# A fused retention and SwiGLU kernel: the last three down-projections by seven products in place of eight

## The chip, the cores and the metric

The kernel runs on one core of one Trainium2 chip. The metric is the device time of one execution in microseconds (us). Before the change it is 229.09 us, the median of three runs (229.01 to 229.27). The profile is one execution of the same program, with a span of 227.3 us from its first to its last instruction.

The engines are named as the profile names them: PE is TensorE (PEld its weight loads), DVE is VectorE, ACT is ScalarE, POOL is GpSimd, SP is SyncE, which here only issues DMAs (SPq).

## What is computed

A retention layer (a decayed running state per head) whose output goes through an RMS norm and a gated feed-forward layer. Sizes: 4 sequences, 8 heads, 768 positions, head size 64; then 3072 tokens of 512 features, with 1536 hidden features.

```python
for t in range(S):
    state = gamma * state + einsum('bhd,bhe->bhde', k[:, :, t], v[:, :, t])
    y[:, :, t] = scale * einsum('bhd,bhde->bhe', q[:, :, t], state)
x = y.transpose(0, 2, 1, 3).reshape(3072, 512)
xn = x / sqrt(mean(x * x, -1) + 1e-6) * rms_g
g, val = xn @ w_gate, xn @ w_val            # 512 -> 1536
out = (g * sigmoid(g) * val) @ w_out        # 1536 -> 512
```

## The kernel before

The sequence of 768 positions is cut into 6 groups of 128 positions; a group holds all 4 sequences, so 512 tokens. For each group the kernel makes the retention output, the norm, and the feed-forward layer, and work of neighbouring groups is interleaved.

The order of all of it is written out in one string, ORDER. Each word is one small operation: its name, its group, its sequence or pair of sequences and its parts; after "/" the PSUM banks (0 to 7) that it writes, after "@" the engine. The words are issued in that order, each engine works through its own in order, and a layer below puts in semaphores where one operation needs another's data or its buffer. The words that matter here:

- Retention of groups 2 to 5, by pairs of sequences: k multiplies keys and values into kv_ps (L485), u0 and u1 add it to the state (VectorE, L490 and L494), b0 and b1 cast the state. z starts y_ps with the state (L506), a makes the scores a_ps (L462), m0 and m1 mask them into am (VectorE, L471), and w adds scores times values to y_ps (L522, L506).
- Norm: S squares and sums y_ps on ScalarE (L567), R makes rstd on GpSimd (L581, L583), N makes xn on VectorE (L595), and XE transposes it by a DMA from SP's queue into xnT (L614). y_ps keeps its bank until N has read it.
- Feed-forward: g and v are products of 4 matmuls of 512 columns for one slice of 128 hidden features (L665), s the silu on ScalarE (L676), h the product of both on VectorE into hT (L686 for groups 2 to 5). hT holds the 1536 hidden features as 12 slices of 128 by 512 tokens.
- Down-projection: d multiplies 128 tokens of hT with w_out, 12 matmuls of 512 columns into one bank (L695), so 48 matmuls a group; e does the last 128 tokens of group 5 in three pieces of 192, 192 and 128 columns (L721). o copies the bank to o_sb on ScalarE or VectorE (L142), and st stores it from SP's queue (L710, L712).
- V, Cq: scaled copies of the values and queries as they arrive (L383, L364), on VectorE or GpSimd.

In the order of before, the down-projections of groups 2 and 3 stand between group 4's w and its first g, where the norm and the transposes of group 4 run on the other engines.

Of the kernel before, what the change touches and what calls it, by code (L numbers as in the profile page):

```python
# [54 lines left out]
v.2.6.7.0.4/4 g.2.7.8.0.4/5 g.2.5.6.0.4/3 g.2.4.5.0.4/6 v.2.1.2.0.4/0 R.3.0 R.3.1 h.2.6.7.0.4 N.3.1 Cq.3.2@P
h.2.1.2.0.4 N.3.0 V.3.2@P s.2.8.9.0.4 s.2.7.8.0.4 s.2.5.6.0.4 g.2.0.1.0.4/5 v.2.7.8.0.4/1 v.2.8.9.0.4/2 v.2.5.6.0.4/3
g.2.2.3.0.4/0 k.3.1/47 tq.3.3 tk.3.3 tk.3.2 Lv.4.2@S tq.3.2 Lv.5.2@S Lq.5.3@S XE.3.1@S Lq.4.0@S Cq.5.3@P V.4.2@D
h.2.5.6.0.4 h.2.7.8.0.4 u0.3.1 h.2.8.9.0.4 s.2.4.5.0.4 s.2.2.3.0.4 b0.3.1@A s.2.0.1.0.4 v.2.0.1.0.4/3 v.2.4.5.0.4/1
v.2.2.3.0.4/2 z.3.1/50 a.3.1/46 u1.3.1 h.2.4.5.0.4 m0.3.1 m1.3.1 h.2.0.1.0.4 Cq.5.2@D h.2.2.3.0.4 g.2.10.11.0.4/1
v.2.9.10.0.4/4 w.3.1 g.2.9.10.0.4/3 v.2.11.12.0.4/6 v.2.10.11.0.4/2 g.2.11.12.0.4/7 S.3.2 s.2.9.10.0.4 S.3.3  # L60
s.2.10.11.0.4 s.2.11.12.0.4 Lk.4.3@P R.3.2 R.3.3 N.3.2 h.2.9.10.0.4 N.3.3 h.2.10.11.0.4 h.2.11.12.0.4 Lv.5.3@S
XE.3.0@S tq.4.1 Lv.4.0@S st.0.0@S XE.3.2@S Lv.4.1@S XE.3.3@S st.0.1@S Lv.4.3@S Lq.4.2@S d.2.1.0.10/4 d.2.1.10.12
d.2.2.0.12/6 d.2.3.0.12/2 g.3.11.12.0.4/7 v.3.0.1.0.4/0 g.3.0.1.0.4/1 g.3.6.7.0.4/5 g.3.10.11.0.4/3 st.0.3@S Lq.4.3@S
tk.4.0 st.1.0@S o.2.3@A s.3.6.7.0.4 o.2.2@A s.3.0.1.0.4 V.5.3@D o.2.1@A V.4.3@D h.3.0.1.0.4 V.4.1@P s.3.11.12.0.4
s.3.10.11.0.4 g.3.3.4.0.4/5 g.3.2.3.0.4/6 v.3.11.12.0.4/4 v.3.10.11.0.4/3 v.3.6.7.0.4/7 g.3.4.5.0.4/0 v.3.3.4.0.4/1
g.3.1.2.0.4/2 Cq.4.3@D h.3.10.11.0.4 h.3.11.12.0.4 V.4.0@D h.3.6.7.0.4 s.3.3.4.0.4 s.3.4.5.0.4 s.3.1.2.0.4 Cq.4.2@P
# [30 lines left out]
def kernel(  # L97
# [11 lines left out]
    nc = tc.nc  # L109
# [88 lines left out]
    def ring(shape, dtype, name, bufs):  # L198
        return sb.tile(shape, dtype, name=name, bufs=bufs)
# [506 lines left out]
    def st(e, bk, c, b, i=None):  # L706
# [4 lines left out]
        else:  # L711
            e.dma_start(out=out_h[c, b // 2, b % 2][:, :, m], in_=x)  # L712


    CUT = (0, 192, 384, 512)

    @op
    def e(e, bk, c, b, i):
# [42 lines left out]
```

## Time and profile before

| what | us |
|---|---|
| median of three runs | 229.09 |
| span of the profiled execution | 227.3 |
| PE busy | 221.2 |
| DVE busy | 121.5 |
| ACT busy | 88.0 |
| POOL busy | 88.2 |

A row of the chain is: start, length, engine, tile and line, with the count of merged instructions. A row of the timeline is: start, length, engine, line, operation and its tiles. A row of a group ends with its busy time, the mean length of one instruction in ns, and the idle time in front of it with what ended that. How busy PE and DVE were in 40 equal slices of the span, in tenths:

```profile
PE   7899999999999999999999999999999999999994
DVE  6495459946388685247751377850564543052211
```

### The profile page before, as it was taken

Reading aid. Unit: us, or ns where it says so; the run is one execution under the profiler, and the core shown is the slowest. Engines: PE = TensorE matmul, PEld = TensorE weight load, DVE = VectorE, ACT = ScalarE, POOL = GpSimd, SP = SyncE. Lnnn points to the kernel's source line nnn. Section 1 sums busy time; section 2 is a strip of 40 time slices with the busy share of each in tenths; the row PEclk is TensorE's granted clock in tenths of the full one; section 3 lists DMA queues with packets and bytes.
Section 4 is the critical chain, followed back from the end, with each engine's and each line's share of the span. In section 5 each row is a group of like instructions: output and inputs, shape, how many; then the busy total and the mean of one; then the engine's idle time right before and its main releaser. Section 6 shows DMA issues by size and latency. Waiting matters only on the chain.

```text
span 227.3 us, 5786 instructions
## 1 busy us (share of the span) xinstructions
PE 221.2 (97%) x2410; PEld 115.0 (51%) x2410; DVE 121.5 (53%) x224; ACT 88.0 (39%) x192; POOL 88.2 (39%) x137
## 2 busy tenths in 40 slices
PE   7899999999999999999999999999999999999994
PEld 2577854565455644444444445544554444444453
DVE  6495459946388685247751377850564543052211
ACT  7798323341525540724411545251452232152011
POOL 8899897746632640743225803170031000000000
PEclk9999999999999999999999999999999999999999
DMA  6999999999999986999969999556003400220116
GB/s 130 174 164 180 197 172 193 177 187 200 186 145 159 182 119 146 248 143 219 154 163 257 163 159 218 130 102 136 2 6 87 144 0 4 91 92 0 46 52 227
DMA packets 105355, 31.57 MB, mean 139 GB/s; under 512 B 94449, under 2 KB 102385, under 8 KB 105330
## 3 DMA queue, kind: packets, MB, share of 16 engines
q0 software_dynamic: 40112, 9.70, 46.4%
q1 hardware_dynamic: 65218, 21.51, 44.1%
q8 instruction: 19, 0.31, 0.6%
q14 instruction: 6, 0.05, 0.1%
HBM read 28.31 MB, written 6.29 MB: 152 GB/s over the span
## 4 chain that ended last, share of the span: by engine, by line
PE 87%; DMA 4%; DVE 2%; issue 2%; POOL 2%; SPq 0%; ACT 0%; POOLq 0%
PE g_ps L665 26%; PE v_ps L665 26%; PE o_ps L695 25%; DMA qb<-in_q_dram 2%; DMA qf<-in_q_dram 2%; PE o_ps L721 1%; DVE am L535 1%; PE kv_ps L485 1%; PE a_ps L428 1%; PE y_ps L522 1%; PE y_ps L506 1%; PE y_ps L550 1%; PE t_ps L396 1%; PE t_ps L391 1%; PE xt_ps L608 1%
## 5 line engine op out<-in xcount | busy, mean ns | idle before, releaser
L665 PE MATMUL v_ps<-xnT,wv_b 128*128 128x512 bf16 (+2 forms) x344 | 70.0, 345 | 0.0
L665 PE MATMUL g_ps<-xnT,wg_b 128*128 128x512 bf16 (+2 forms) x344 | 69.7, 345 | 0.0
L676 ACT ACTIVATE sg<-g_ps 128x512 bf16<-128x512 f32 (+2 forms) x76 | 41.9, 577 | 67.0 <-PE g_ps L665 54.4
L695 PE MATMUL o_ps<-wo_b,hT 128*128 128x512 bf16 x276 | 62.6, 380 | 0.0
L686 DVE TENSOR_TENSOR hT<-sg,v_ps 128x512 bf16<-128x512 bf16 x48 | 32.8, 723 | 38.7 <-ACT sg L676 19.4
L665 PEld LDWEIGHTS <-wv_b 128*128 128x128 bf16 x344 | 30.8, 98 | 30.2 <-DVE hT L686 0.4
L665 PEld LDWEIGHTS <-wg_b 128*128 128x128 bf16 x344 | 30.3, 98 | 29.3 <-DVE st_f L494 0.2
L695 PEld LDWEIGHTS <-hT 128*128 128x128 bf16 x276 | 26.2, 98 | 29.8
L595 DVE SCALAR_TENSOR_TENSOR xn<-y_ps,rstd,g_bc 128x512 bf16<-128x512 f32 x24 | 17.6, 746 | 12.7 <-POOL rstd L583 12.1
L688 DVE TENSOR_TENSOR hT<-sg,v_ps 128x512 bf16<-128x512 bf16 (+2 forms) x28 | 16.6, 606 | 14.6 <-PE v_ps L665 7.5
L364 POOL TENSOR_TENSOR qb<-qf,ydec 128x512 bf16<-128x512 f32 x13 | 13.7, 1065 | 26.9 <-DMA qf<-in_q_dram 26.9
L142 ACT COPY o_sb<-o_ps 128x512 f32<-128x512 f32 (+2 forms) x17 | 9.2, 553 | 36.6 <-PE o_ps L695 32.3
L567 ACT ACTIVATE xsq<-y_ps 128x512 f32<-128x512 f32 x24 | 14.2, 596 | 21.6 <-PE y_ps L506 16.2
L336 POOL DMA_DIRECT2D kb<-in_k_dram x20 | 18.2, 911 | 2.6 <-DMA wo_b<-in_moe_w_out_dram 1.4
L581 POOL TENSOR_SCALAR ms<-ssq 128x1 f32<-128x1 f32 x21 | 4.4, 212 | 35.1 <-ACT xsq L567 30.0
L471 DVE TENSOR_TENSOR am<-a_ps,causal_h 128x512 bf16<-128x512 f32 x16 | 10.6, 684 | 8.9 <-PE a_ps L462 8.9
L142 DVE COPY o_sb<-o_ps 128x512 f32<-128x512 f32 (+1 forms) x9 | 5.7, 647 | 13.8 <-PE v_ps L665 4.8
L583 POOL TENSOR_TENSOR rstd<-ms,mhalf 128x1 f32<-128x1 f32 x21 | 11.6, 551 | 1.7
L535 DVE TENSOR_TENSOR am<-a_ps,mask 128x512 bf16<-128x512 f32 x16 | 10.2, 681 | 2.4 <-PE a_ps L428 2.3
L383 POOL TENSOR_TENSOR vp<-vf,vdec 128x512 bf16<-128x512 f32 x7 | 7.3, 1050 | 7.9 <-DMA vf<-in_v_dram 7.9
L383 DVE TENSOR_TENSOR vp<-vf,vdec 128x512 bf16<-128x512 f32 x9 | 6.2, 692 | 4.5 <-DMA vf<-in_v_dram 4.5
L229 PE MATMUL hot_ps<-one 128*128 128x512 bf16 x16 | 6.2, 523 | 1.0 <-DVE one L149 1.0
(99 smaller groups left out, 166.4 us busy)
## 6 DMA issues: line engine op xcount, KB each, us to landing
out_dram<-o_sb SPq DMA_DIRECT2D x23, 256.0 KB, 2.4
vf<-in_v_dram SPq DMA_DIRECT2D x17, 256.0 KB, 3.6
qf<-in_q_dram SPq DMA_DIRECT2D x16, 256.0 KB, 4.1
kb<-in_k_dram POOLq DMA_DIRECT2D x23, 128.0 KB, 6.1
wo_b<-in_moe_w_out_dram POOLq DMA_DIRECT2D x3, 512.0 KB, 10.7
qb<-in_q_dram POOLq DMA_DIRECT2D x8, 128.0 KB, 7.4
vp<-in_v_dram POOLq DMA_DIRECT2D x7, 128.0 KB, 10.1
wv_b<-in_moe_w_val_dram POOLq DMA_DIRECT2D x3, 256.0 KB, 6.2
```

Source lines behind the costliest of these rows:

```text
L142: return (e.copy if e is ACT else e.tensor_copy)(out, in_)
L336: i = done[n, c, b] = e.dma_start(out=x, in_=rows[n][b, c])
L364: e.tensor_tensor(out=u["qb"], in0=u["qf"], in1=ydec[:, c, :, None].to_broadcast([128, H, D]), op=ALU.mult)
L383: e.tensor_tensor(out=u["vp"], in0=u["vf"], in1=vdec[:, c, :, None].to_broadcast([128, H, D]), op=ALU.mult)
L535: return DVE.tensor_tensor(out=u["am"][:, i], in0=u["a"][i], in1=m, op=ALU.mult)
L567: return ACT.activation(xsq, flat(u["y"]), AF.Square, accum_out=u["ssq"])
L595: return DVE.scalar_tensor_tensor(out=u["xn"], in0=flat(u["y"]), scalar=u["rstd"], in1=g_bc, op0=ALU.mult, op1=ALU.mult)
L665: r = nc.tensor.matmul(p[:, (n - n0) * m:(n - n0 + 1) * m], W[w][0][:, s, n * 128:(n + 1) * 128], xnT[c][:, s, b0 * C:b1 * C], start=s == ...
L676: return ACT.activation(sg[:, :cols], done["wg", c, n0, b0][:, :cols], AF.Silu)
L686: return DVE.tensor_tensor(out=out, in0=sg, in1=p, op=ALU.mult)
L688: return DVE.tensor_tensor(out=hT[c][:, n0:n1, b0 * C:b1 * C], in0=sg, in1=p, op=ALU.mult)
L695: nc.tensor.matmul(o_ps[c, b], hT[c][:, n, b * C:(b + 1) * C], wo_b[:, n, :], start=n == 0, stop=n == NFF - 1)
```

## The change

For groups 3, 4 and 5 the down-projection C = A B (A: 512 tokens by 1536, B: w_out, 1536 by 512) is cut into two by two blocks: A into halves of 256 tokens and of 768 features, B into halves of 768 features and of 256 columns. Strassen's scheme, in Winograd's form, makes the four blocks of C from seven block products in place of eight:

- Sums of B (word tw, once): T1 = B12 - B11, T2 = B22 - T1, T3 = B22 - B12, T4 = B21 - T2. Each is 1536 elements a partition.
- Sums of A (word ss, for each group, in parts by slices): S1 = A21 + A22, S2 = S1 - A11, S3 = A11 - A21, S4 = A12 - S2. S3 and S4 are written over A21 and A12 in hT, S1 and S2 into a buffer, ssum. In groups 3 and 4 a part is 3 slices by 256 tokens (768 elements), in group 5 2 slices (512).
- Products (word p): P1 = A11 B11, P2 = A12 B21, P3 = S4 B22, P4 = A22 T4, P5 = S1 T1, P6 = S2 T2, P7 = S3 T3. Each is 12 matmuls of 256 columns (6 slices by two blocks of 128 tokens); in group 5 each is issued in two halves of 6, by token block.
- Three banks hold the results (word r). P1 is copied out by ScalarE (part), then P2 is added in its bank, which gives C11, copied to o_sb by ScalarE. P6's bank is read with P1 added (part), then takes P7, is read with P1 added (part), then takes P4, and gives C21. P5's bank gives C22, then takes P3 and gives C12. So P2 waits for the copy of P1, P7 and P4 for the two reads of P6's bank, P3 for the reading of C22. These reads are additions on VectorE.

All sums of A and B are bf16 in and out, on VectorE. The sums of B lie where the masks of groups 0 and 1 lay, ssum where their states lay, the parts in other buffers used early. The list ORDER is word for word the same up to group 2's down pieces, but with bank numbers exchanged (1 with 7, 2 with 6, 3 with 5); after that it is written anew. Four of the last eight stores, of 256 columns each, are issued by ScalarE.

```diff
+    def tw(e, bk, i):
+        b11, b12, b21, b22 = (wo_b[:, f, m] for f in (F0, F1) for m in (M0, M1))
+        out, x, y = ((t1, b12, b11), (t2, b22, t1), (t3, b22, b12), (t4, b21, t2))[i - 1]
+        return e.tensor_tensor(out=out, in0=x, in1=y, op=ALU.subtract)
...
+    def ss(e, bk, i, c, n0, n1):
+        (a11, a21), (a12, a22) = ([hT[c][:, f, m] for m in (slice(0, GT // 2), slice(GT // 2, GT))] for f in (slice(n0, n1), f1))
+        out, x, y, f = ((s1, a21, a22, ALU.add), (s2, s1, a11, ALU.subtract), (a21, a11, a21, ALU.subtract),
+                        (a12, a12, s2, ALU.subtract))[i - 1]
+        return e.tensor_tensor(out=out, in0=x, in1=y, op=f)
...
+    def p(e, bk, i, c, j0=0, j1=2, n0=0, n1=NFF // 2):
+        for n in range(n0, n1):
+            l, off, r = {1: (h0, 0, w0[:, :, M0]), 2: (h1, 0, w1[:, :, M0]), 3: (h1, 0, w1[:, :, M1]), 4: (h1, k, t[:, 3]),
+                         5: (None, 1, t[:, 0]), 6: (None, 2, t[:, 1]), 7: (h0, k, t[:, 2])}[i]
+            for j in range(j0, j1):
+                nc.tensor.matmul(x[:, j - j0], z[:, j * C:(j + 1) * C], r[:, n],
+                                 start=i in (1, 5, 6) and n == 0 and j == j0, stop=n == NF2 - 1, skip_group_check=True)
...
+    def r(e, bk, i, c, j0=0, j1=2, j=None):
+        z = {6: 1, 67: 1, 21: 1, 22: 67, 12: 6}.get(i)
+        if i in (1, 6, 67):
+            return copy(e, y, x) if i == 1 else DVE.tensor_tensor(out=y, in0=x, in1=z, op=ALU.add)
+        for n in range(j0, j1):
+            if i == 11:
+                copy(e, y, x[:, n - j0])
+            else:
+                DVE.tensor_tensor(out=y, in0=x[:, n - j0], in1=z[:, n - j0], op=ALU.add)
```

VectorE between the last hT of group 3 and the first hT of group 4, before (am is m0 and m1, xn the norm, both of groups 4 and 5):

```order
L686 TENSOR_TENSOR hT<-sg,v_ps 128x4x2x64 x3
L471 TENSOR_TENSOR am<-a_ps,causal_h 128x512 x2
L595 SCALAR_TENSOR_TENSOR xn<-y_ps,rstd,g_bc 128x512 x4
L364 TENSOR_TENSOR qb<-qf,ydec 128x512
L471 TENSOR_TENSOR am<-a_ps,causal_h 128x512
L490 TENSOR_TENSOR st_m_109<-st_f_107,kv_ps 128x512
L471 TENSOR_TENSOR am<-a_ps,causal_h 128x512
L142 COPY o_sb<-o_ps 128x512
```

And now, up to the last xn of group 4 and the addition behind it:

```order
L692 TENSOR_TENSOR hT<-sg,v_ps 128x4x2x64 x3
L759 TENSOR_TENSOR ssum<-hT 128x768 x2
L759 TENSOR_TENSOR hT<-hT 128x3x256
L477 TENSOR_TENSOR am<-a_ps,causal_h 128x512 x2
L759 TENSOR_TENSOR ssum<-ssum,hT 128x768 x2
L759 TENSOR_TENSOR hT<-hT,ssum 128x3x256
L601 SCALAR_TENSOR_TENSOR xn<-y_ps,rstd,g_bc 128x512
L759 TENSOR_TENSOR hT<-hT,ssum 128x3x256
L788 TENSOR_TENSOR part_3039<-p_ps,part_2936 128x512
L759 TENSOR_TENSOR hT<-hT 128x3x256
L601 SCALAR_TENSOR_TENSOR xn<-y_ps,rstd,g_bc 128x512 x3
L788 TENSOR_TENSOR part_3101<-p_ps,part_2936 128x512
```

All eight sums of group 3 and its first two additions now stand ahead of or between the masks and norms of group 4. On TensorE the same place holds, in this order: P1, z and a of group 4's second pair, P2, w of both pairs, P6, ten matmuls of group 2's d, P7, P5, P4, z and a of group 5, P3, the last two matmuls of that d, w of group 5, then the first g of group 4.

VectorE at the end of the program, before (the last hT of group 5, then copies of the down-projection):

```order
L686 TENSOR_TENSOR hT<-sg,v_ps 128x4x2x64 x11
L142 COPY o_sb<-o_ps 128x512
L686 TENSOR_TENSOR hT<-sg,v_ps 128x4x2x64 x9
L142 COPY o_sb<-o_ps 128x192
L142 COPY o_sb<-o_ps 128x512 x2
```

And now, from the third sum behind the last hT:

```order
L759 TENSOR_TENSOR ssum<-ssum,hT 128x512
L759 TENSOR_TENSOR hT<-hT,ssum 128x2x256 x2
L788 TENSOR_TENSOR part_3039<-p_ps,part_2936 128x256
L759 TENSOR_TENSOR hT<-hT,ssum 128x2x256
L759 TENSOR_TENSOR hT<-hT 128x2x256
L788 TENSOR_TENSOR part_3039<-p_ps,part_2936 128x256
L788 TENSOR_TENSOR part_3101<-p_ps,part_2936 128x256
L797 TENSOR_TENSOR o_sb<-p_ps,part_3101 128x256
L788 TENSOR_TENSOR part_3101<-p_ps,part_2936 128x256
L797 TENSOR_TENSOR o_sb<-p_ps,part_3101 128x256
L797 TENSOR_TENSOR o_sb<-p_ps,part_2936 128x256 x2
L797 TENSOR_TENSOR o_sb<-p_ps,part_3039 128x256 x2
```

Where three copies ended the program, seven sums (two stand ahead of the first row here) and ten additions follow the last hT. On TensorE, 14 half products follow the last v: P1, P1, P2, P2, P6, P6, P5, P7, P7, P5, P4, P4, P3, P3. The down-projection of group 4, which stood there before, is done earlier.

More of the change, by code (lines that the diff above doesn't have):

```diff
@@ new lines @@
+XE.0.0@A g.0.0.2.0.1/2 X.0.1/5 v.0.0.2.0.1/4 Y.0.3/7 tab s.0.0.2.2.3 S.0.3 U.0.0.2@A U.0.2.2@A s.0.0.2.0.1 XE.0.1@D
+Lq.1.1@P R.0.3 h.0.0.2.2.3 h.0.0.2.0.1 N.0.3 mc.0@P g.0.4.5.0.3/5 g.0.5.6.0.3/0 g.0.0.2.1.2/1 v.0.5.6.0.3/6
+v.0.4.5.0.3/2 v.0.0.2.1.2/4 g.0.2.3.0.3/3 X.0.3/7 Lq.1.0@P Lq.1.2@P Lk.1.1@P B.0.1 wg.6.9 Lk.1.3@P s.0.4.5.0.3
+s.0.5.6.0.3 h.0.4.5.0.3 h.0.5.6.0.3 zst.0@P s.0.2.3.0.3 XE.0.3@D s.0.0.2.1.2 v.0.2.3.0.3/2 g.0.3.4.0.3/3 v.0.0.4.3.4/1
+g.0.4.6.3.4/7 g.0.0.4.3.4/6 h.0.0.2.1.2 D.1.0@D h.0.2.3.0.3 s.0.0.4.3.4 s.0.3.4.0.3 s.0.4.6.3.4 v.0.4.6.3.4/2
@@ L93 @@
+ss.3.5.4.6@D r.6.5.1.2 st.5.1.0@S p.5.5.0.1/7 p.7.5.0.1 r.67.5.0.1 p.7.5.1.2 r.22.5.0.1 p.5.5.1.2/3 st.5.0.0@A
+st.5.2.1@A r.67.5.1.2 p.4.5.0.1 r.22.5.1.2 st.5.3.1@A r.21.5.0.1 p.4.5.1.2 p.3.5.1.2 st.5.2.0@S p.3.5.0.1 r.21.5.1.2
+st.5.3.0@S r.12.5.1.2 st.5.1.1@A r.12.5.0.1 st.5.0.1@S
 """
@@ L167 @@
     darg = const.tile([128, NCH, H], F32, name="darg")
-    below = const.tile([128, C], F32, name="below")
     eps = const.tile([128, 1], F32, name="eps")
@@ L172 @@
     ydec = const.tile([128, NCH, H], F32, name="ydec")
-    mask0 = const.tile([128, 2, NHP, C], F32, name="mask0")
-    mask1 = const.tile([128, 2, NHP, C], F32, name="mask1")
-    qdec = const.tile([128, NHP, C], F32, name="qdec")
-    row_m = const.tile([128, C], F32, name="row_m")
+    shared = NFF // 2 * DM
+    early = const.tile([128, shared], F32, name="early", tag="shared")
+    mask0, mask1 = (early[:, i * H * C:(i + 1) * H * C].rearrange("p (i hp c) -> p i hp c", i=2, hp=NHP) for i in range(2))
+    qdec = early[:, 2 * H * C:2 * H * C + NHP * C].rearrange("p (hp c) -> p hp c", hp=NHP)
+    row_m, below = (early[:, 2 * H * C + (NHP + i) * C:2 * H * C + (NHP + i + 1) * C] for i in range(2))
     lngp = const.tile([128, NHP], F32, name="lngp")
@@ L187 @@
     causal_h = const.tile([128, HC], BF16, name="causal_h")
-    st_b = [const.tile([128, NHP, 2 * D], BF16, name=f"st_b{b}") for b in range(B)]
+    st_all = const.tile([128, 6, NHP, 2 * D], BF16, name="st_b", tag="shared_st")
+    st_b = [st_all[:, b] for b in range(B)]
     t = {(c, b): {} for c in range(NCH) for b in range(B)}
@@ L196, in bank, with ring @@
         return psum.tile(shape, dtype, name=name, tag=f"bank{i}")
-    def ring(shape, dtype, name, bufs):
-        return sb.tile(shape, dtype, name=name, bufs=bufs)
+    def ring(shape, dtype, name, bufs, tag=None):
+        return sb.tile(shape, dtype, name=name, bufs=bufs, tag=tag or name)
     def after(i, *what):
@@ L712, in st @@
             e.dma_start(out=out_h[c, b // 2, b % 2][:, :, m], in_=x)
-    CUT = (0, 192, 384, 512)
-    @op
-    def e(e, bk, c, b, i):
-        p = o_ps[c, b, i] = bank(bk[0], [128, CUT[i + 1] - CUT[i]], F32, "o_ps")
-        for n in range(NFF):
-            nc.tensor.matmul(p, hT[c][:, n, b * C:(b + 1) * C], wo_b[:, n, CUT[i]:CUT[i + 1]],
-                             start=n == 0, stop=n == NFF - 1)
+    NF2 = NFF // 2
+    F0, F1 = slice(0, NF2), slice(NF2, NFF)
+    M0, M1 = slice(0, DM // 2), slice(DM // 2, DM)
@@ new lines @@
+    CUT = (0, DM // 2, DM)
+    sums, prod = {}, {}
+    @op
+    def tw(e, bk, i):
+        if "T" not in sums:
+            sums["T"] = const.tile([128, 4, NF2, DM // 2], BF16, name="wsum", tag="shared")
+        b11, b12, b21, b22 = (wo_b[:, f, m] for f in (F0, F1) for m in (M0, M1))
+        t1, t2, t3, t4 = (sums["T"][:, j] for j in range(4))
+        out, x, y = ((t1, b12, b11), (t2, b22, t1), (t3, b22, b12), (t4, b21, t2))[i - 1]
+        return e.tensor_tensor(out=out, in0=x, in1=y, op=ALU.subtract)
@@ new lines, in row_sum, with part @@
+    def row_sum(i, c, n0, n1):
+        if "S" not in sums:
+            sums["S"] = const.tile([128, 2, NF2, GT // 2], BF16, name="ssum", tag="shared_st")
+        return sums["S"][:, i - 1, n0:n1]
+    def part(i):
+        if ("s", i) not in prod:
+            pool, tag = {1: (sb, "kf"), 6: (const, "shared_g"), 67: (const, "part")}[i]
+            prod["s", i] = pool.tile([128, 2, DM // 2], F32, name=f"part{i}", bufs=1, tag=tag)
+        return prod["s", i]
+    @op
+    def ss(e, bk, i, c, n0, n1):
+        f1 = slice(NF2 + n0, NF2 + n1)
+        (a11, a21), (a12, a22) = ([hT[c][:, f, m] for m in (slice(0, GT // 2), slice(GT // 2, GT))] for f in (slice(n0, n1), f1))
+        s1, s2 = row_sum(1, c, n0, n1) if i < 3 else None, row_sum(2, c, n0, n1) if i != 3 and i > 1 else None
+        out, x, y, f = ((s1, a21, a22, ALU.add), (s2, s1, a11, ALU.subtract), (a21, a11, a21, ALU.subtract),
+                        (a12, a12, s2, ALU.subtract))[i - 1]
+        return e.tensor_tensor(out=out, in0=x, in1=y, op=f)
@@ new lines @@
+    INTO = {1: 1, 2: 1, 11: 1, 6: 2, 7: 2, 4: 2, 67: 2, 21: 2, 5: 3, 3: 3, 22: 3, 12: 3}
+    @op
+    def p(e, bk, i, c, j0=0, j1=2, n0=0, n1=NFF // 2):
+        if bk:
+            prod[INTO[i], c, j0] = bank(bk[0], [128, j1 - j0, DM // 2], F32, "p_ps")
+        x, t = prod[INTO[i], c, j0], sums["T"]
+        h0, h1 = hT[c][:, :NF2], hT[c][:, NF2:]
+        w0, w1 = wo_b[:, :NF2], wo_b[:, NF2:]
+        k = GT // 2
+        for n in range(n0, n1):
+            l, off, r = {1: (h0, 0, w0[:, :, M0]), 2: (h1, 0, w1[:, :, M0]), 3: (h1, 0, w1[:, :, M1]), 4: (h1, k, t[:, 3]),
+                         5: (None, 1, t[:, 0]), 6: (None, 2, t[:, 1]), 7: (h0, k, t[:, 2])}[i]
+            z = row_sum(off, c, n, n + 1)[:, 0] if l is None else l[:, n, off:off + k]
+            for j in range(j0, j1):
+                nc.tensor.matmul(x[:, j - j0], z[:, j * C:(j + 1) * C], r[:, n],
+                                 start=i in (1, 5, 6) and n == 0 and j == j0, stop=n == NF2 - 1, skip_group_check=True)
@@ new lines, in r @@
+    @op
+    def r(e, bk, i, c, j0=0, j1=2, j=None):
+        x = prod[INTO[i], c, j0]
+        if j is not None:
+            x, j0, j1 = x[:, j - j0:j - j0 + 1], j, j + 1
+        z = {6: 1, 67: 1, 21: 1, 22: 67, 12: 6}.get(i)
+        z = z and part(z)[:, j0:j1]
+        if i in (1, 6, 67):
+            y = part(i)[:, j0:j1]
+            return copy(e, y, x) if i == 1 else DVE.tensor_tensor(out=y, in0=x, in1=z, op=ALU.add)
+        for n in range(j0, j1):
+            b = 2 * (i // 10 - 1) + n
+            if ("o", c, b) not in done:
+                done["o", c, b] = ring([128, DM], F32, "o_sb", 6)
+            y = done["o", c, b][:, (M0, M1)[i % 10 - 1]]
+            if i == 11:
+                copy(e, y, x[:, n - j0])
+            else:
+                DVE.tensor_tensor(out=y, in0=x[:, n - j0], in1=z[:, n - j0], op=ALU.add)
```

145 lines of the change are left out of this document (71 added, 74 removed).

## The prediction

> **What bounds the kernel now.** I read the page first (engine shares, slices), then TensorE's waits, then the chain that ended last in order of time, then instruction groups by shape and the timeline.
>
> ```profile
> PE 221.2 (97%) x2410; PEld 115.0 (51%) x2410; DVE 121.5 (53%) x224; ACT 88.0 (39%) x192; POOL 88.2 (39%) x137
> PEclk9999999999999999999999999999999999999999
> ```
>
> TensorE (PE) is busy 97% of the span at full granted clock; VectorE (DVE) is half idle. Are the gaps in TensorE real waits? Its waits, whole list:
>
> ```profile
> PE t_ps L391 <- DMA qb<-in_q_dram: 1.1, 1, 1.1
> PE hot_ps L229 <- DVE one L149: 1.0, 1, 1.0
> PE kv_ps L485 <- DVE vp L383: 0.4, 1, 0.4
> ```
>
> 2.5 us in three waits; the last, for vp, lies at 82 us (first row below), ahead of the stretch that changes. So from group 2 on the time is the length of TensorE's stream, and any microsecond taken out of it shows, as long as no new wait comes in. The chain (start, length) gives its prices:
>
> ```profile
> 81.64 0.66 DVE vp L383
> ...
> 144.52 0.38 PE y_ps L522 x32
> 144.90 0.27 PE y_ps L506 x32
> 145.16 0.32 PE a_ps L462 x32
> ...
> 148.68 10.47 PE o_ps L695 x48
> ...
> 184.16 1.73 PE v_ps L665 x8
> ...
> 215.68 0.99 PE o_ps L721 x12
> 216.66 5.61 PE o_ps L695 x26
> 222.28 1.67 PE o_ps L721 x24
> 223.97 0.27 ACT o_sb L142
> ```
>
> A group's down-projection is 48 matmuls 512 wide: 10.47 us, 218 ns each. One v or g product (4 matmuls) is 0.86 us. Twelve matmuls 192 wide take 0.99 us, 82.5 ns each; the last row is twelve of 192 and twelve of 128, so 128 wide is (1.67 - 0.99)/12 = 57 ns.
>
> **TensorE's part.** Three groups go from 48 matmuls of 512 columns to 7 products of 12 matmuls of 256. No row is 256 wide. Between the 192 and 512 rows the slope is (218 - 82.5)/320 = 0.42 ns a column, which puts 256 at 109.6 ns; half of a 512 is 109. So 84 x 109.6 = 9.21 us, a saving of 1.26 us a group, **3.8 us** for three (3.6 to 3.9). Group 5's narrow pieces (0.99 + 1.67 = 2.66 against 12 x 0.218 = 2.62) return 0.04 more. A product is 1.32 us; in group 5, cut in halves, 0.66.
>
> ```profile
> L695 PEld LDWEIGHTS <-hT 128*128 128x128 bf16 x276 | 26.2, 98 | 29.8
> ```
>
> The loading of weights could spoil this, since there are now 84 loads in place of 48. A load's record is 98 ns long beside a 512, but the 192-wide row already issues one each 82.5 ns, so loads hide at 109. The Trainium skill (TensorE: Matmul & The Clock Gate, section Back-to-back issue gap) speaks against the change: it gives a sustained stream 81 ns at 128 wide and 131 at 512, hence about 98 at 256 as an estimate, by which 84 x 98 = 8.2 us would replace 48 x 131 = 6.3. The trace disagrees at both ends, 57 and 218 ns, and the rows decide.
>
> **VectorE's part.** Added are 4 sums of weights (1536 elements a partition), 16 sums of activations of 768 and 12 of 512, all two-byte in SBUF; then 22 additions of 256 and 4 of 512 that read PSUM. Four copies go.
>
> ```profile
> L142 DVE COPY o_sb<-o_ps 128x512 f32<-128x512 f32 x8 | 5.5, 683 | 9.5 <-PE v_ps L665 4.8 <-PE o_ps L695 4.7
> L142 DVE COPY kT<-t_ps 128x512 bf16<-128x512 bf16 x2 | 0.8, 420 | 0.5 <-PE t_ps L396 0.5
> L650 DVE TENSOR_TENSOR st_f<-st_f,kv_ps 128x256 f32<-128x256 f32 x2 | 0.8, 416 | 0.0
> L650 DVE TENSOR_TENSOR st_f<-st_f,kv_ps 128x512 f32<-128x512 f32 x1 | 0.7, 679 | 0.0
> ```
>
> The additions that read PSUM have their rows: 416 and 679 ns, so 22 x 0.416 + 4 x 0.68 = 11.9 us. Those two rows give 1.03 ns an element and 153 ns fixed. No row has a two-input sum with all operands two-byte, so two ends. Upper: the same rate, 0.94 us for 768, 0.68 for 512, 1.73 for 1536, 30 us in all. Lower: the same copy takes 683 ns in four-byte and 420 in two-byte; (420 - 153)/512 = 0.52 ns an element, so 0.55, 0.42 and 0.95 us, 17.7 us in all. Every row at the high rate has a four-byte operand, and the new sums have none, so I take the **lower end** and keep the other as a rival. The Trainium skill (VectorE: DVE Perf Modes, section The perf-mode tier table) has bf16 tensor_tensor in SBUF at twice the fp32 rate, 1224 against 2293 ns for 2048 elements, which as an estimate is 0.56 us for 768 and leads to the same sum; no run here shows it yet.
>
> ```profile
> 120.00:227.00 107.00, 103.94 (x959) 49.95 (x956) 44.19 (x67) 34.55 (x71) 18.59 (x30) 1.00 0.52 100
> ```
>
> Net of the copies (2.4 us) that is 27 us more. From 120 us on VectorE was busy 44 of 107 us (third figure of the row); 71 fits, but it works in order, so place decides.
>
> ```profile
> 115.87 0.67 DVE L383 TENSOR_TENSOR vp<-vf,vdec 128x512 bf16<-128x512 f32 x1
> 120.66 0.69 DVE L383 TENSOR_TENSOR vp<-vf,vdec 128x512 bf16<-128x512 f32 x1 [4.12 <-DMA vf<-in_v_dram]
> 127.28 0.73 DVE L686 TENSOR_TENSOR hT<-sg,v_ps 128x512 bf16<-128x512 bf16 x1 [5.93 <-ACT sg L676]
> ...
> 131.29 0.67 DVE L383 TENSOR_TENSOR vp<-vf,vdec 128x512 bf16<-128x512 f32 x1
> ...
> 138.51 1.95 DVE L686 TENSOR_TENSOR hT<-sg,v_ps 128x512 bf16<-128x512 bf16 x3 [0.31 <-PE v_ps L665]
> ```
>
> The first three rows show where VectorE idled, the last that the gaps between two starts are shorter than the records: three hT products in 1.95 us, about 0.61 a start. I count 0.48 us a start for a 768-sum, 0.34 for a 512-sum, and the full length where a result is waited for.
>
> - *Sums of weights.* They come where VectorE idled 4.1 + 5.9 us; 3.8 (upper end 6.9) fits. Cost nothing.
> - *Group 3's products*, counted from the end of its last v product (zero). TensorE: P1 to 1.32, z and a of group 4 (16 matmuls of L506 and 32 of L462, some 0.5 by the first rows) to 1.8. P2 adds into P1's bank and must wait for ScalarE's copy (0.59 us by the row below, 1.37 to 1.96): 0.15 lost. P2 ends at 3.3, w.4.0 (32 of L522, 16 of L506, 0.5) at 3.8, then w.4.1 needs the second mask product. VectorE: last hT from 0.1, three sums from 0.9, mask products from 2.35 to 3.65. Just in time. The norm then goes w, ScalarE square, GpSimd rstd, VectorE xn:
>
> ```profile
> L142 ACT COPY o_sb<-o_ps 128x512 f32<-128x512 f32 x15 | 8.6, 588 | 33.3 <-PE o_ps L695 32.3 <-DMA out_dram<-o_sb 0.9
> ```
>
> ```profile
> 146.24 0.20 ACT L567 ACTIVATION_READ_ACCUMULATOR xsq<-y_ps 128x1 f32 x1
> 147.40 0.75 DVE L595 SCALAR_TENSOR_TENSOR xn<-y_ps,rstd,g_bc 128x512 bf16<-128x512 f32 x1 [0.49 <-POOL rstd L583]
> 152.36 1.06 POOL L364 TENSOR_TENSOR qb<-qf,ydec 128x512 bf16<-128x512 f32 x1
> 152.77 1.19 DVE L364 TENSOR_TENSOR qb<-qf,ydec 128x512 bf16<-128x512 f32 x1
> ```
>
> ```profile
> L614 SPq DMA_TRANSPOSE xnT<-xn x8: 1189/1215/1711, 149.1 to 176.0; - x8
> DMA to landing us min/median/max: 2.3/2.4/3.6
> ```
>
>   From the end of the accumulator's read to xn is 0.96 us, and the four xn now stand between sums: I get starts at 5.5, 7.7, 8.4 and 9.0. P5's bank holds the third one's y_ps, free at 9.15, wanted at 9.1. After the last xn (9.8) two transposes of about 1.2 us in SP's queue and their landing (2.3 to 3.6, the last row) end at 13.3 to 14.6; TensorE asks for xnT at 14.8. All in all **0.5 us** of stalls (0.2 to 1.5).
> - *Group 4's products* have v and g products of group 5 between them: P2 comes 1.7 us after P1, P7 2.6 us after P6. No stall.
> - *Group 5's products* stand alone at the end, 14 halves of 0.66, 9.2 us. After the last hT (0.1 to 0.8) VectorE has seven sums and one addition ahead of the first P7, which is the eighth half, at 4.6; its last S3 ends at 4.5. P4, at 6.6, wants an addition done at 5.8; the last P3 one done at 7.1, and starts at 7.9. No stall.
> - *The end.* An addition of 256 (0.42) takes the place of a copy of 128 (0.27), and the last store is 128 KB in place of 64; stores of 64, 96 and 256 KB landed 1.9, 2.0 and 2.4 us after issue, so 0.2 more. Together +0.35.
>
> ```profile
> out_dram<-o_sb SPq DMA_DIRECT2D x8, 256.0 KB, 2.4
> out_dram<-o_sb SPq DMA_DIRECT2D x2, 96.0 KB, 2.0
> out_dram<-o_sb SPq DMA_DIRECT2D x1, 64.0 KB, 1.9
> ```
>
> ScalarE loses 8 copies of 512 and two small ones and gets 2 of 512 and 8 of 256, about 1 us less; the four stores it issues stand behind all its other work, so nobody waits for them. The shared buffers reuse space that groups 0 and 1 left long before.
>
> **Sum:** -3.8 - 0.04 + 0.5 + 0.35 = -3.0 us. The profiled span was 227.3 us, so 224.3; the median of 229.09 lies 1.8 us around it, which I leave as it is: **226.1 us**.
>
> **Rivals.**
> 1. *Sums at the four-byte rate (slower).* The sums start 0.4 us later each. In group 3 the second mask product ends at 4.8 in place of 3.65, w.4.1 waits 1 us, and the xn, P7 and P5 behind it come later by turns: some 3 us in all. In group 4, P6's second half and P7 wait for S2 and S3, near 1.5. In group 5, P7 waits 0.6. That is 5 us: **231**. It turns into a loss once a 768-sum takes more than about 0.78 us, where 60% of that is lost. For it: every two-input row here runs at that rate. Against: they all have a four-byte operand.
> 2. *The rate holds but VectorE is late anyway.* Just-in-time places in group 3 slip: an operation with two SBUF inputs took 1.19 us on VectorE while GpSimd ran its own (rows of 152 us), against 0.67 without at 131 us, and GpSimd still has two such loads there. One to two sums so delayed and xnT later by as much: +1 to +2.5, **227.8**.
> 3. *A fixed cost a matmul* that the narrow rows, only 12 or 24 long, hide: TensorE gains nothing. 35 ns a matmul more would take the 1.26 us of a group (36 matmuls more); with the stalls and the end **229.9**. For it stand 84 weight loads; against it 57 and 82.5 ns, whose slope (0.40) leaves 6 ns at zero width. The page on TensorE cited above would have it so.
>
> **How the numbers follow.** Forecast 0.62 (225.0 to 226.9), rival 2 0.18 (227 to 228.6), waits that eat all of the gain 0.06 (within 0.2% of before, about what a measurement can tell from no change), rival 1 0.11, rival 3 0.03. Faster 0.80, same 0.06, slower 0.14. The range takes in the forecast and rival 2: 225.0 to 228.6.
>
> **What would show it.** Right: 252 matmuls of 256 columns, near 109 ns apart; sums of 768 near 0.55 us; TensorE's waits still a few, with ScalarE's copy of P1 among them, together under 1 us more; the chain's end an addition and a store. Wrong: sums near 0.9 us with long waits for ssum and am in group 3 and at the end (rival 1); waits of g_ps for xnT or of P5 for xn at the start of group 4 (rival 2); 84 matmuls taking over 10 us without waits (rival 3).

## The result and the profile after

The changed kernel took **226.32 us**, the median of four runs, beside 229.05 for four runs of the kernel before on the same chip. The ratio is 0.9869 with a 95% interval of 0.9838 to 0.9901, so 3.0 us less (2.3 to 3.7); the medians differ by 2.7. The forecast was 226.1 (225.0 to 228.6). One of the four runs took 230.26: late runs turn up with either list (two of six when the changed kernel ran again, two of eleven of the kernel before beside it), and the ratios leave them out while the medians do not.

The first lines of the page of after, busy time, share and count of each engine, then the granted clock:

```profile
PE 215.6 (96%) x2466; PEld 123.7 (55%) x2494; DVE 148.1 (66%) x278; ACT 87.1 (39%) x192; POOL 88.6 (40%) x137
...
PEclk9999999999999999999999999999999999999998
```

TensorE still fills the span (223.9 us now, 227.3 before), but with 5.6 us less work by the records (28 matmuls of after have none, as the counts of PE and PEld show, so this is somewhat too much). VectorE has 26.6 us more of it; the prediction counted 27. All of TensorE's waits, in us, times, longest:

```profile
PE hot_ps L235 <- DVE one L154: 1.0, 1, 1.0
PE t_ps L397 <- DMA qb<-in_q_dram: 1.0, 1, 1.0
PE o_ps L701 <- issue: 0.6, 4, 0.2
PE v_ps L671 <- issue: 0.3, 2, 0.2
PE kv_ps L491 <- DVE vp L389: 0.3, 1, 0.3
```

The three old waits are there. No wait for a sum, an addition, a mask, a norm or a transpose has come in. New are six short "issue" gaps, together 0.9 us. They are no idle time: in front of each stands a matmul without a record. At 158.1 us, for instance, two weight loads of a d run on PEld, and only one matmul of it is on record (start, length):

```profile
158.07 0.11 PEld L701 LDWEIGHTS <-hT 128*128 128x128 bf16 x2
```

```profile
158.30 0.38 PE L701 MATMUL o_ps<-wo_b,hT 128*128 128x512 bf16 x1 [0.16 <-issue]
```

The chain in order of time (start, length) shows where TensorE's stream changed: group 3's products, group 4's, and the end.

```profile
113.72 5.18 PE o_ps L701 x24
...
144.03 1.31 PE p_ps L776 x12
145.85 0.41 PE y_ps L528 x32
146.42 1.42 PE p_ps L776 x12
147.84 0.37 PE y_ps L528 x32
148.34 1.42 PE p_ps L776 x12
149.81 2.11 PE o_ps L701 x9
151.92 3.93 PE p_ps L776 x36
156.09 0.26 PE a_ps L468 x32
156.35 1.42 PE p_ps L776 x12
...
183.86 1.34 PE p_ps L776 x12
...
186.93 2.62 PE p_ps L776 x24
...
192.14 5.24 PE p_ps L776 x48
...
211.19 9.19 PE p_ps L776 x84
220.40 0.42 DVE o_sb L797
```

Three readings. First, group 5's 84 matmuls of 256 columns took 9.19 us without a break, 109.4 ns each; the forecast had 109.6. Second, in group 3 three of the products took 1.42 us in place of 1.31, and each of those stands right behind small matmuls (y_ps or a_ps, 64 by 64). Third, the first y_ps L528 stands *before* the second p_ps: w of group 4's first pair runs ahead of P2. The sentence ahead of the prediction, that P2 precedes w of both pairs, is wrong, and so is the place of P2 in the prediction's walk through group 3.

The kernel's front part does not change, yet its length differs from profile to profile (113.7 us in after and 114.4 in before, but 118.5 in slow_sums and 116.7 in keys_early, whose profiled executions took 237.72 and 228.64 us). So the profiles are compared by a **stretch**: from the first matmul of group 2's first d to the end of the last matmul. Its start in the chain of before (its last row, 222.28 with 1.67, stands in the prediction):

```profile
114.41 7.77 PE o_ps L695 x36
```

Before: 222.28 + 1.67 - 114.41 = 109.54 us, and 3.35 from there to the end of the span. After: 211.19 + 9.19 - 113.72 = 106.66, and 3.52. So the stretch gained 2.88 and the end lost 0.17, together 2.71. (The span is printed to 0.1 us; by the records as they are kept, the two ends are 3.40 and 3.52 us, so 0.12 lost.) The medians differ by 2.73, the ratio gives 3.0; neither is known well enough to tell 2.7 from 2.8. The other 0.7 us of the spans' difference lies in the front part and belongs to the two executions, not to the change.

Of the groups of instructions of VectorE (form, count, busy us, mean ns, idle us before them), the new ones:

```profile
L797 DVE TENSOR_TENSOR o_sb<-p_ps,part 128x256 f32<-128x256 f32 x18 | 7.1, 422 | 3.9 <-PE p_ps L776 3.8
...
L788 DVE TENSOR_TENSOR part<-p_ps,part 128x512 f32<-128x512 f32 x4 | 2.7, 685 | 1.8 <-PE p_ps L776 1.8
L739 DVE TENSOR_TENSOR wsum<-wo_b,wsum 128x1536 bf16<-128x1536 bf16 x2 | 2.6, 1320 | 0.1
...
L759 DVE TENSOR_TENSOR ssum<-hT 128x768 bf16<-128x768 bf16 x4 | 2.1, 555 | 0.1
...
L739 DVE TENSOR_TENSOR wsum<-wo_b 128x1536 bf16<-128x1536 bf16 x2 | 1.9, 946 | 0.0
...
L759 DVE TENSOR_TENSOR ssum<-hT 128x512 bf16<-128x512 bf16 x3 | 1.3, 423 | 0.1
```

The sums run at the two-byte rate that the prediction chose: 555, 423 and 946 ns against its 0.55, 0.42 and 0.95 us; the additions out of PSUM (422, 685) are those of the rows that it took them from (416, 679). The Trainium skill (VectorE: DVE Perf Modes, section The perf-mode tier table) gave 0.56 us for 768 by the prediction's estimate, and the trace agrees. Of the pair of weight sums with a mean of 1320 ns, one took 0.96 us and the other 1.68.

### The profile page after: what moved, and what is told of

It reads as the page before. It is cut to its first block, busy times and chain, and to the rows that moved or that the text cites. A ratio compares the mean times of both kernels' runs of the same rounds, so it can differ in the third digit from the quotient of the medians.

```text
span 223.9 us, 5994 instructions
## 1 busy us (share of the span) xinstructions
PE 215.6 (96%) x2466; PEld 123.7 (55%) x2494; DVE 148.1 (66%) x278; ACT 87.1 (39%) x192; POOL 88.6 (40%) x137
## 4 chain that ended last, share of the span: by engine, by line
PE 85%; DVE 4%; DMA 4%; issue 2%; SPq 1%; ACT 1%; POOL 1%; POOLq 0%; ACTq 0%
PE v_ps L671 27%; PE g_ps L671 26%; PE p_ps L776 12%; PE o_ps L701 9%; DMA qb<-in_q_dram 2%; DMA out_dram<-o_sb 2%; PE kv_ps L491 1%; DVE am L541 1%; PE y_ps L512 1%; PE y_ps L528 1%; PE a_ps L434 1%; DVE xn L601 1%; PE a_ps L468 1%; PE y_ps L556 1%; PE t_ps L402 1%
## 5 line engine op out<-in xcount | busy, mean ns | idle before, releaser
L692 DVE TENSOR_TENSOR hT<-sg,v_ps 128x512 bf16<-128x512 bf16 x48 | 33.9, 725 | 26.3 <-PE v_ps L671 21.0
L701 PE MATMUL o_ps<-wo_b,hT 128*128 128x512 bf16 x136 | 32.0, 379 | 0.8 <-issue 0.6
L701 PEld LDWEIGHTS <-hT 128*128 128x128 bf16 x144 | 13.4, 98 | 14.4
L776 PEld LDWEIGHTS <-hT 128*128 128x128 bf16 x180 | 17.4, 98 | 3.4
L776 PE MATMUL p_ps<-wo_b,hT 128*128 128x256 bf16 x108 | 13.1, 273 | 0.0
L541 DVE TENSOR_TENSOR am<-a_ps,early 128x512 bf16<-128x512 f32 x16 | 10.2, 685 | 2.3 <-PE a_ps L434 2.1
L797 DVE TENSOR_TENSOR o_sb<-p_ps,part 128x256 f32<-128x256 f32 x18 | 7.1, 422 | 3.9 <-PE p_ps L776 3.8
L776 PE MATMUL p_ps<-wsum,ssum 128*128 128x256 bf16 x72 | 8.9, 273 | 0.0
```

The costliest lines, as they stand in the source:

```text
L541: return DVE.tensor_tensor(out=u["am"][:, i], in0=u["a"][i], in1=m, op=ALU.mult)
L692: return DVE.tensor_tensor(out=out, in0=sg, in1=p, op=ALU.mult)
L701: nc.tensor.matmul(o_ps[c, b], hT[c][:, n, b * C:(b + 1) * C], wo_b[:, n, :], start=n == 0, stop=n == NFF - 1)
L776: nc.tensor.matmul(x[:, j - j0], z[:, j * C:(j + 1) * C], r[:, n], start=i in (1, 5, 6) and n == 0 and j == j0, stop=n == NF2 - 1, skip_gr ...
```

## The experiments

The stretch and what follows it, from the chain of each kernel's one profile; "changes" counts, in the list of each kernel from group 2's first d on, how often TensorE goes from 64 by 64 matmuls to full ones. "Rest" is good to 0.05 us.

| kernel | median us | ratio to before, interval | changes | stretch | rest |
|---|---|---|---|---|---|
| before | 229.05 | | 7 | 109.54 | 3.35 |
| after | 226.32 | 0.9869 (0.9838 to 0.9901) | 10 | 106.66 | 3.52 |
| again (after, once more) | 227.0 | 0.9907 (0.9888 to 0.9927) | 10 | 106.53 | 3.50 |
| slow_sums | 232.84 | 1.0174 (1.0157 to 1.019) | 10 | 113.69 | 3.49 |
| no_row_sums | 226.13 | 0.9892 (0.9867 to 0.9918) | 10 | 106.55 | 3.53 |
| stores_sp | 226.51 | 0.99 (0.987 to 0.9931) | 10 | 106.54 | 3.47 |
| g5_plain | 228.07 | 0.9956 (0.993 to 0.9983) | 10 | 107.90 | 4.18 |
| g3_plain | 229.15 | 1.0014 (0.9991 to 1.0037) | 8 | 109.77 | 3.46 |
| regroup | 226.75 | 0.9906 (0.9879 to 0.9932) | 8 | 106.92 | 3.48 |
| switches | 227.72 | 0.9935 (0.9908 to 0.9962) | 14 | 107.73 | 3.50 |
| keys_early | 225.94 | 0.9864 (0.9831 to 0.9897) | 9 | 106.36 | 3.49 |

The four profiles whose TensorE does the same in the same order (after, again, no_row_sums, stores_sp) agree in the stretch within 0.13 us, so it tells apart what the times, with intervals of some 0.3% to each side, cannot.

### The changed kernel again

> The changed kernel once more, nothing edited, to see the spread of its runs: one of its first four was 230.3 us, the others 225.5 to 226.8. If that one was a disturbance that can hit any program, most runs lie within 225.3 to 227 and the runs of before scatter as much; if the change made the kernel depend on when a load lands, runs near 230 come again, about one in four, and before shows none.

No edit. 227.0 us, ratio 0.9907; the interval overlaps the first one. The gain stands. What was asked of the spread is answered with the result.

### The rate of the sums

```diff
-        return e.tensor_tensor(out=out, in0=x, in1=y, op=f)
+        return e.scalar_tensor_tensor(out=out, in0=x, scalar=1.0, in1=y, op0=ALU.mult, op1=f)
```

> The 28 sums of activations (not those of weights) are written as a scalar_tensor_tensor (times 1.0, then add or subtract), same result. If that form runs at the four-byte rate, a 768-sum takes 0.94 us in place of 0.55. The walk of the prediction then gives about +5 us (waits of TensorE for the mask products and sums in group 3, some 3; in group 4 some 1.5; at the end 0.6): 230 to 232. The rival view, that VectorE has room enough and the order hides the sums, gives +1 or less: under 227.5.

232.84 us: slower than before by 1.7%, and 6.5 us over the changed kernel, above the 230 to 232 that were expected. VectorE's timeline (start, length) behind the last hT of group 3, and the three longest of TensorE's new waits (us, times, longest):

```profile
149.71 1.83 DVE L759 SCALAR_TENSOR_TENSOR ssum<-hT 128x768 bf16<-128x768 bf16 x2
...
152.32 1.28 DVE L477 TENSOR_TENSOR am<-a_ps,causal_h 128x512 bf16<-128x512 f32 x2
```

```profile
PE p_ps L776 <- DVE hT L692: 1.5, 2, 0.8
PE p_ps L776 <- DVE ssum L759: 1.1, 2, 0.8
...
PE y_ps L528 <- DVE am L477: 0.8, 2, 0.4
```

The same sums in a form that ran at the four-byte rate (two in 1.83 us, 0.88 from start to start with a record of 0.95) turn the gain into a loss. This is the first rival, made to happen: the second mask product ends at 153.60, and w, P6, P7, P5, group 4's products and the end of the program wait in turn. Counted from the start of the stretch and against again, group 3's products end 3.0 us late (some 3 expected), group 4's add 2.3 (1.5) and group 5's 1.8 (0.6): the expectation had group 3 right and the two later places too small. The three rows are 3.4 us; four more, for part, hT, st_f and xn (0.5 to 0.6 each), bring the new waits to 5.6. So the change rests on the two-byte rate, and VectorE's time matters as soon as it is late.

### The sums left out

```diff
-                         5: (None, 1, t[:, 0]), 6: (None, 2, t[:, 1]), 7: (h0, k, t[:, 2])}[i]
+                         5: (h1, k, t[:, 0]), 6: (h0, 0, t[:, 1]), 7: (h0, k, t[:, 2])}[i]
```

and all 28 ss words go out of the list.

> Leaves out all 28 sums of activations (the products read blocks of hT as they are, so the output is another), TensorE's work stays. If VectorE's lateness holds TensorE up anywhere, this shows by how much: by the forecast 0.2 to 0.5 us less (225.8 to 226.1). If the missing part of the gain is only TensorE's own (narrow matmuls, changes between small and full tiles), no change within 0.2 us. If VectorE is what limits (rival 2), 1 us or more less.

226.13 us, and a stretch of 106.55 against 106.53 to 106.66. VectorE lost about 12 of its 148 us and TensorE gained nothing: at the two-byte rate no sum of activations delays anything. Together with the run before, this brackets the cost of the sums: 0 at 0.55 us, 6.5 us at 0.95.

### One group put back

Group 5 in plain form, its sums, products and additions taken out of the list:

```diff
-ss.*.5 p.*.5 r.*.5 st.5.*
+d.5.0.0.12/7 o.5.0@A st.5.0@S d.5.1.0.12/4 o.5.1@D st.5.1@A d.5.2.0.12/1 o.5.2@A st.5.2@S d.5.3.0.12/3 o.5.3@A st.5.3@S
```

> Group 5's down-projection as 48 matmuls of 512 columns again, groups 3 and 4 by seven products. If the gain is TensorE's columns, group by group, it loses 1.3 us (10.47 against 9.19), less 0.1 to 0.3 since a full-width store and copy at the end replace an addition: +0.9 to +1.4 us on the changed kernel. If the end gains nothing from the scheme (additions and stores take it back), +0.3 or less.

228.07 us. Expected was +0.9 to +1.4 on the changed kernel; it is +1.75. The stretch grows by 1.24 us against after, near what TensorE's columns give: 48 matmuls of 512 at 216 ns are 10.36 us against 9.19. The rest grows by 0.66, since a whole bank of 512 columns and a store of 256 KB now come last. There the expectation had the sign wrong: the full-width copy and store give nothing back. Group 5's part of the gain is thereby measured: all that its columns promise.

Group 3 in plain form:

```diff
-p.1.3/7
+d.3.0.0.12/7 o.3.0@A
-p.6.3/1
+d.3.1.0.12/1 o.3.1@A
-p.7.3
+d.3.2.0.12/7 o.3.2@D
-p.4.3
+d.3.3.0.12/3 o.3.3@A
```

with its ss, r and other p words taken out.

> Group 3's down-projection as 48 matmuls of 512 columns in the same places between group 4's retention work, groups 4 and 5 by seven products. By columns +1.3 us; group 3 is where the sums stand ahead of masks and norms, so if those cost TensorE waits, plain is only +0.5 to +0.9 us. If rival 2 were at work there, 0 or less.

229.15 us, stretch 109.77: 3.1 us over after, far more than a group's columns and than any of the expected values. The chain says why this is no clean price:

```profile
160.30 0.33 PE a_ps L468 x32
160.63 0.68 DVE am L477
...
208.97 0.40 issue
209.37 0.47 DVE hT L692
```

Group 3's products had kept TensorE busy in the places where masks and hT of the next groups are made. With other work in these places, waits for am (0.9 and 0.7 us in TensorE's waits) and for hT came in. The run shows that the new list fits the new products, and leaves open what group 3's share is alone.

### The last stores

```diff
-st.5.0.0@A st.5.2.1@A
+st.5.0.0@S st.5.2.1@S
...
-st.5.3.1@A
+st.5.3.1@S
...
-st.5.1.1@A
+st.5.1.1@S
```

> The four stores that ScalarE issues at the end go back to SP's queue. An issue takes 0.6 us there and the eight stores become ready over 6 us, the last four within 2 us: the last would start about 0.3 us later if the queue backs up, so 0 to +0.4 us. A view in which two queues matter for the bandwidth of the stores gives +0.5 or more.

226.51 us, 3.47 us behind the last matmul against 3.52. The queue that issues the four stores makes no difference that shows.

### What a change of tile size costs

The gain in columns is larger than what arrived (worked out below), and TensorE waited for nobody. What remains are the rows of 1.42 us, 0.11 more than 1.31. The short gap ahead of one of them is no part of it: 147.84 + 0.37 ends at 148.21 and the next product starts at 148.34, but the last 16 small matmuls of w run in between. TensorE's timeline of after has them (start, length; the records of neighbours overlap), and they end at 148.34:

```profile
148.04 0.30 PE L512 MATMUL y_ps<-st_h,qT 64*64 64x64 bf16 x16
```

The second cost lies on the other side, where small matmuls follow full ones. In the chain of before, 16 of these matmuls take 0.13 us behind other small ones and 0.25 behind full ones:

```profile
148.55 0.13 PE y_ps L506 x16
...
159.15 0.25 PE y_ps L506 x16
```

So by these rows going to small matmuls and back costs TensorE 0.12 + 0.11 = 0.23 us. The expectations of the runs below count only the 0.11, or (keys_early) take the time of w's 16 matmuls for the second cost; that its 0.25 comes near the 0.23 is luck. Two lists with other counts of changes were tried, then a third.

Fewer changes (regroup), by joining small matmuls:

```diff
-k.4.0/52
-u0.4.0
-u1.4.0
...
-k.4.1/65 u0.4.1
+k.4.0/54 k.4.1/62 u0.4.0 u1.4.0 u0.4.1
...
-k.5.1/2
-u0.5.1
...
-a.4.0/67
+a.4.0/67 k.5.1/4 u0.5.1
...
-p.3.3
+k.5.0/4 p.3.3
...
-k.5.0/0
```

> Same work, three small kv products moved next to other small ones (the first pair's beside the second's, one beside z and a, the last ahead of P3), in banks that are free. TensorE then changes twice less from small tiles (64 wide) to full ones. If each such change costs 0.11 us as the rows of both traces suggest (12 matmuls take 2.70 behind a small one and 2.59 elsewhere), 0.2 to 0.3 us less; if that 0.11 is only in how ends are modelled, no change within 0.1 us in TensorE's stretch from group 2's first d to the end.

A miss: 226.75 us, stretch 106.92, 0.26 to 0.4 longer instead of shorter. The chain shows waits that the moves themselves brought:

```profile
136.59 0.58 DVE st_m L496
...
137.94 0.61 DVE st_m L496
```

Both key-value products at one place give VectorE their state updates in one piece, and a v product then waits for them (0.5 us). With shorter delays elsewhere, waits take 0.8 us of the stretch; the two changes less give back 0.4, summed over the places where TensorE changes. So the price of a change holds here too, and the waits are what the expectation missed.

More changes (switches), by cutting four runs of small matmuls in two:

```diff
-p.1.3/7 z.4.1/32
+p.1.3.0.2.0.3/7 z.4.1/32 p.1.3.0.2.3.6
-p.4.3 z.5.1/25
+p.4.3.0.2.0.3 z.5.1/25 p.4.3.0.2.3.6
-v.4.8.9.0.4/3 z.5.0/65
+z.5.0/65 v.4.8.9.0.4/3
-k.5.1/2 v.3.6.7.0.4/3
+v.3.6.7.0.4/3 k.5.1/2
```

> Same work, four changes more from small tiles to full ones (P1 of group 3 split around z, P4 split around z of group 5, z of group 5's first pair a v earlier, one kv product behind a v). At 0.11 us each +0.4 us; if they cost nothing, within 0.15 us.

227.72 us, stretch 107.73: 1.07 us over after for four more changes, 0.27 each, and more than the 0.4 that was expected. TensorE's list of waits is that of after, but the chain has VectorE's last hT ahead of the first z that was moved, and there 16 small matmuls take 0.54 us in place of 0.25. Without this 0.29 a change costs 0.20 to 0.23. Around the first cut product:

```profile
144.41 0.74 DVE hT L691
145.19 0.31 PE y_ps L511 x14
145.51 0.76 PE p_ps L775 x6
```

Six matmuls of 256 are 0.66 by the forecast's price, and took 0.76: the 0.11 again.

One change fewer (keys_early), the part of regroup that brought no wait:

```diff
-p.3.3
+k.5.0/4 p.3.3
...
-k.5.0/0
```

> One move alone: group 5's first key-value product (k.5.0, 16 small matmuls) goes from behind P3 of group 3 to behind the small matmuls ahead of P3, so that from group 2's first down piece on TensorE changes nine times from small matmuls to full ones in place of ten. Theory (each such change costs TensorE about 0.25 us: some 0.13 of a gap ahead of the first full matmul, as in the rows 147.84 + 0.37 and then 148.34, and 0.11 in its length, 1.42 in place of 1.31 for twelve): the stretch from the first d of group 2 to the last matmul, 106.53 to 106.66 us in the five profiles with the changed list, comes to 106.3 to 106.45, the time to 226.1 (225.4 to 227.2), no difference from the changed kernel that the times alone can show. Rival (the cost lies not in the changes but in the places, since waits that the profile calls issue sit there): the stretch stays at 106.5 to 106.7. Other rival (the bank that it takes, 4, comes free too late): a wait of kv_ps or of the matmuls behind it, and the stretch grows to 106.8 or more.

The stretch is 106.36, 0.17 us under the lowest of the four alike ones, and inside the range that was expected of the theory; it is one profile, and the four alike ones differ by 0.13 among themselves. 225.94 us, ratio 0.9864: beside the changed kernel the times show no difference. So from 9 to 10 changes the stretch grows by 0.17 to 0.30 us, and from 10 to 14 by 1.07 to 1.20, of which 0.29 is the wait of z.

## Why the prediction was right, by its steps

| term | forecast us | measured us |
|---|---|---|
| TensorE's columns, three groups, with group 5's narrow pieces | -3.84 | -3.57 |
| waits in group 3 | +0.5 | 0 to 0.1 |
| changes of tile size | not seen | +0.6 to +0.7 |
| the end | +0.35 | +0.12 to +0.17 |
| sum | -3.0 | -2.7 |

*What bounds the kernel*: right. TensorE's stream sets the time before and after; less work on VectorE (no_row_sums) or another queue (stores_sp) did not move it, more on VectorE (slow_sums) did where TensorE came to wait.

*TensorE's columns*: right in mechanism, 0.27 us too large. The 109.6 ns a matmul came true (109.4). The 218 ns on the other side of the subtraction was too high: it was 10.47 / 48 from a row that begins with a change of tile size. A row of before inside the feed-forward part has none:

```profile
185.89 2.59 PE o_ps L695 x12
```

That is 216 ns, so 10.36 us a group. Groups 3 and 4 then save 10.36 - 9.19 = 1.17 and 10.36 - 9.20 = 1.16 (1.34 + 2.62 + 5.24 = 9.20 in the chain of after), group 5 10.43 - 9.19 = 1.24, together 3.57.

*Stalls in group 3*: half right. VectorE's walk held within 0.4 us: the four xn were forecast at 5.5, 7.7, 8.4 and 9.0 us after the last v product's end (144.03). VectorE's timeline of after:

```profile
149.12 0.74 DVE L601 SCALAR_TENSOR_TENSOR xn<-y_ps,rstd,g_bc 128x512 bf16<-128x512 f32 x1
...
151.31 2.06 DVE L601 SCALAR_TENSOR_TENSOR xn<-y_ps,rstd,g_bc 128x512 bf16<-128x512 f32 x3
```

They start at 5.1, and from 7.3 on. Nothing waited for them. Of the 0.5 us, the prediction's walk gives a place only to 0.15 at P2 and 0.05 at P5; the rest was allowance. The small loss forecast for P2 could not occur, since w of the first pair stands between P1 and P2 and covers ScalarE's copy. That error and the unseen changes nearly cancel, by luck: 0.5 us of waits were forecast, and 0.69 us of something else were paid.

*What was paid instead*: the stretch gained 2.88 where the columns give 3.57. The rest is 0.69 us. The new list has three more changes from small to full matmuls. Their price can be added up place by place from the ends of TensorE's records. Each first product behind small matmuls is 0.11 us longer, seven times before and ten times now: 0.32 us more. The 480 small matmuls of the stretch are the same in both lists, but in ten runs in place of seven they take 5.48 us in after and 5.37 in again, against 5.09 before: 0.28 to 0.39 more. (The 0.11 between after and again is w at 145.85 us, which took 0.41 where again has 0.29; why is not known.) Together this is 0.60 to 0.71, so the three added changes carry the 0.69, but for 0.1 that after's profile alone has. Lists with 9 and 14 changes show about the same price: 0.17 to 0.30 for one change, 0.20 to 0.23 for each of four. Why a change costs this is not shown: TensorE running empty, or a first load of weights that no longer hides behind a matmul (the prediction's row has 98 ns for a load), would look alike here. The Trainium skill (TensorEngine Tiling (Array Packing), section Tiling Modes, Key Properties) states that a change of tiling mode drains TensorE. It gives no price. The trace agrees that a change costs time, 0.23 us there and back, and does not show that draining is the cause. The prediction weighed another page against the change and missed this rule.

*Sums of weights and of activations*: right. Cost nothing at the two-byte rate, as no_row_sums shows for those of activations; those of weights lie before 130 us where TensorE shows no wait for them.

*Groups 4 and 5*: right. No stall in either; group 5's 84 matmuls are one unbroken row.

*The end*: less than half of the forecast, 0.12 to 0.17 us. The addition is 0.15 us longer than the copy (0.42 and 0.27 in the chains). Of the last stores, in the DMA issues of after (count, size, median us to landing):

```profile
out_dram<-o_sb ACTq DMA_DIRECT2D x4, 128.0 KB, 2.1
out_dram<-o_sb SPq DMA_DIRECT2D x4, 128.0 KB, 2.0
```

One of 128 KB takes 0.1 us more than the 64 KB one before, where 0.2 was forecast.

*The rivals*. The first (four-byte rate) fell, and slow_sums shows that its mechanism and its sign were right: forecast +5 us, measured +6.5. Of the second (contention with GpSimd) a part occurred, in one weight sum of 1.68 us, where nobody waited, and in GpSimd's rstd (last section). The third (a fixed cost a matmul) fell by the 109.4 ns; a cost did come up, but for each change of tile size, not for each matmul.

## What to carry to other kernels

Where TensorE's stream is the time, count not only its columns but how often it goes between small tiles and full matmuls: each change cost about as much as one matmul of 512 columns here, and no wait in the profile names it. Take the price of a matmul from a row in the middle of its kind, since a row that begins behind another kind carries the change in it. Work for another engine that stands beside the bound is free only at the rate at which it fits: the same 28 sums cost nothing at 0.55 us and 6.5 us at 0.95, so find out which form of an instruction runs at which rate before counting on it.

## What the runs showed of the hardware

The price of a change of tile size was not expected. Nor was how differently two instructions for the same sum run: TENSOR_TENSOR 555 ns and SCALAR_TENSOR_TENSOR 954 ns for 768 two-byte elements in SBUF.

```profile
L759 DVE SCALAR_TENSOR_TENSOR ssum<-hT 128x768 bf16<-128x768 bf16 x4 | 3.7, 954 | 0.1
```

VectorE and GpSimd ran slower side by side, each in its turn. The second of the two weight sums with a mean of 1320 ns, and GpSimd's operation beside it (start, length):

```profile
117.75 1.68 DVE L739 TENSOR_TENSOR wsum<-wo_b,wsum 128x1536 bf16<-128x1536 bf16 x1
```

```profile
117.32 1.30 POOL L389 TENSOR_TENSOR vp<-vf,vdec 128x512 bf16<-128x512 f32 x1 [4.06 <-DMA vf<-in_v_dram]
```

The sum with the same number of elements at 115.77 took 0.95 and the first of the two, at 116.76, took 0.96; the second began while GpSimd's operation ran and took 1.68. That GpSimd is the cause here was not tried. In group 3, where VectorE's sums run, GpSimd's rstd took 0.76 us twice, the first time here, and 0.55 later (150.61):

```profile
147.73 0.76 POOL L589 TENSOR_TENSOR rstd<-ms,mhalf 128x1 f32<-128x1 f32 x1
```

Here the sums are the cause. In again, with the sums, the first two rstd of the group took 0.93 and 0.76 us; in no_row_sums, without them, all four took 0.55, as the first of them shows:

```profile
148.49 0.55 POOL L589 TENSOR_TENSOR rstd<-ms,mhalf 128x1 f32<-128x1 f32 x1
```
